# Block kernel on one core: an attention stage planned with other costs, banks and places for its side work

## The chip, the core and the metric

The kernel runs on one core of one Trainium2 chip, as one launch. The metric is the device time of that launch in microseconds (us). Three runs of the kernel before gave a median of 2030.43 us (2028.11 to 2034.91).

The core's engines run side by side, each through its own list of instructions in order: PE (matrix products; PEld is its loading of weights), DVE and ACT (elementwise work, both of which read the PSUM banks that PE writes), POOL (elementwise work on SBUF alone), and SP, which here issues the DMAs. An instruction that waits holds up everything behind it on its engine.

## The reference

All arithmetic is fp32. `xn` is the normalised input, and the result is `x + s * g`:

```python
x = A_x                                   # [1, 2048, 576]
xn = _layernorm(x, axis=-1)
# s: 32 heads of 18, a query sees itself and the 255 keys before it
q, k, v = heads(xn @ wqkv)
scores = einsum("bhqd,bhkd->bhqk", q, k) * (18 ** -0.5)
p = softmax(where((i - j >= 0) & (i - j < 256), scores, -1e9))
s = tokens(einsum("bhqk,bhkd->bhqd", p, v)) @ wo
# g: a gated MLP with a 2048 x 2048 mix over the tokens
z = gelu(xn @ w_in)                       # 4608 columns
z1, z2 = z[..., :2304], layernorm(z[..., 2304:])
g = silu((z1 * (w_sp @ z2 + b_sp)) @ w_out)
```

## The kernel before, in words

An fp32 factor is split into a high and a low part, and a product is three fast matmuls. ACT writes the high part and DVE or POOL the low part (`split` at line 108; `wq_high` and `wq_low` for the query/key weights; the jobs of `load_z1` for the z1 weights). The stages stand one after the other on PE, in microseconds of the profiled execution:

- 0 to 170: x is loaded in four chunks of four tiles, normalised (`stats_of` makes mean and variance, `scales_of` the factors, `norm_act` the normalised copy on ACT), turned by PE (`turn_group`), and multiplied by nine blocks of query/key weights. `fetch(j)` loads block j of these, three buffers deep. `keep_narrow` splits a product of 256 tokens and stores it with two DMAs.
- 170 to 464: the remaining query/key products, v, and z2. At the end of z2 the first row maxima of the attention are taken between z2's matmuls.
- 464 to 1044: the attention, with z1 as its filling. This is the stage that most of the change is about.
- 1044 to 1106: the product with `wo`. 1106 to 1794: the product of `w_sp` with z2. 1794 to 2028: the product with `w_out` and the result.

**The attention stage.** The work is cut into 16 units: 8 groups of four heads, by 2 halves of the queries. A unit first needs the row maxima. `max_item` (line 578) multiplies 128 queries with up to 384 keys into a bank of the pool `sps`, and DVE takes the masked maximum (line 582). After 32 of them `max_split` and `max_end` turn the maxima, and four small DMAs (line 608, `att<-mhl`) put them beside the queries as two further rows of the operand, so that the next product comes with its maximum already subtracted. Then `scores` (line 702) multiplies a block of keys with up to 384 queries into a bank of the pool `tps`, ACT takes the exponential (line 706), POOL cuts the corners of the mask (lines 714 and 717), and `pv` (line 730) multiplies by v. v holds a column of ones, so a row of each head's result is the denominator. `finish` brings the denominators to 128 partitions by DMA (`den`), DVE inverts them, a DMA writes them to `r_d`, another reads them back, spread over the partitions (`rp<-r_d`, line 774), DVE multiplies by them in two halves (line 781), and four DMAs store the unit (line 791).

Maxima, scores and z1 use half of PE's rows each. Heads 0 and 2 of a group lie in rows 0 to 63, heads 1 and 3 in rows 64 to 127, and two instructions on different halves run side by side. The products with v use all of PE. z1 is 18 blocks of weights (f) by 2 parts of the tokens by 27 matmuls on each half of the rows (`z1_rows`, line 649); a block's raw weights come by one DMA of 576 KB into a single buffer (line 618), and six jobs of ACT and POOL split them.

**What sets the order.** The order of all instructions is written when the program is built. For the attention stage a planner does so: a clock of its own advances by a cost for each instruction (`spend` for PE, `use` for ACT, DVE and POOL). At each step it takes, for the half of PE's rows that is free first, a score or a maximum if its operands and its bank should be there by that clock (`can_score`, `can_max`), and else a z1 matmul (`fill`). DMAs are registered with a due time (`after`) and issued when the clock has reached it (`tick`). `LOAD_NS` and `MAX_NS` are the times after which loaded queries and keys, and maxima, are taken to be there; `DIVIDE_AT` tells when a unit's divisions go in; `GUARD` is a margin of 150 ns. On the chip nothing follows that clock: the engines run their lists as fast as the waits let them.

The last unit's denominators are handled behind the loop, between the first products with `wo`.

## Time and profile before

| what | value |
|---|---|
| median of three runs | 2030.43 us |
| the profiled execution: its time, its span | 2029.56 us, 2027.8 us |
| PE busy, share of the span | 1925.4 us, 95% |
| mean granted clock of PE | 0.963 |
| DVE, ACT, POOL busy | 1061.5, 911.8, 354.8 us |
| attention, 464 to 1030 us: PE busy of 566 us, mean granted clock | 496.9 us, 0.91 |

The times are read from the span's start. A row of the waits names an engine and a line, what it waited for, the total in us, how often and the longest. In the table by stretches each engine has its busy time and in brackets the number of its instructions; PEclk is the mean share of PE's clock that was granted.

### The profile page before, as it was taken

To read this page: it belongs to the slowest core of one execution; us is meant where nothing else is said; L and a number is where in the kernel's file an instruction comes from. 1 tells how busy PE (TensorE), PEld (TensorE's weight loads), DVE (VectorE), ACT (ScalarE), POOL (GpSimd) and SP (SyncE) were. 2 spreads that over 40 slices of the span, in tenths; PEclk is the share of its full clock that TensorE was granted. 3 is DMA by queue.
4 is the path that set the end of the run, shared out by engine and by line. 5 is a ranking of instruction groups with operands and counts; after the bars stand their busy time and mean duration, and the time that the engine had idled before them with its cause. 6 is when DMAs were issued, how large, how long until landed. Compare 5 with 4: busy or idle time off the path is not lost.

```text
span 2027.8 us, 38429 instructions
## 1 busy us (share of the span) xinstructions
PE 1925.4 (95%) x14552; PEld 1654.0 (82%) x14552; DVE 1061.5 (52%) x2305; ACT 911.8 (45%) x1758; POOL 354.8 (17%) x424
## 2 busy tenths in 40 slices
PE   8799999999999878898899999999999999999999
PEld 7699999986676656566689888888888888899998
DVE  6420343556565445555322777756877576753322
ACT  4422322314554345455635856546556544442221
POOL 2222233433343224233410000000000000000000
PEclk8899999999998888989889999999999999999999
DMA  5686688886464644455356867766577655775451
GB/s 184 172 221 178 206 277 283 277 258 177 131 178 118 164 109 120 122 159 145 112 175 241 272 219 245 255 233 228 182 241 245 206 172 186 225 256 169 134 158 55
DMA packets 233353, 389.84 MB, mean 192 GB/s; under 512 B 51024, under 2 KB 144720, under 8 KB 233040
## 3 DMA queue, kind: packets, MB, share of 16 engines
q1 hardware_dynamic: 233168, 387.39, 61.9%
q8 instruction: 114, 1.87, 0.4%
q14 instruction: 71, 0.58, 0.1%
HBM read 274.74 MB, written 111.78 MB: 191 GB/s over the span
## 4 chain that ended last, share of the span: by engine, by line
PE 78%; DMA 9%; DVE 5%; ACT 3%; SPq 2%; issue 2%; POOL 0%; POOLq 0%; DVEq 0%; ACTq 0%
PE acc L1377 30%; PE po L1470 11%; PE mb L200 9%; PE ma L200 6%; PE ma L649 5%; PE mb L649 5%; PE ops L730 4%; PE wops L1137 3%; PE sp L578 2%; PE tps L702 2%; DMA z1raw<-in_w_z_dram 2%; DMA att<-st_d 2%; DVE junk L582 1%; DMA st_d<-qkhl 1%; SPq L346 1%
## 5 line engine op out<-in xcount | busy, mean ns | idle before, releaser
L582 DVE CUSTOM_DVE_ANT_0 junk<-sp,band 128x384 bf16<-128x384 f32 (+1 forms) x512 | 275.8, 539 | 232.5 <-PE sp L578 124.0
L1377 PE MATMUL acc<-spl,zh 128*128 128x512 f32 x1008 | 392.6, 389 | 1.2 <-DVE spl L110 1.0
L1377 PE MATMUL acc<-sph,zl 128*128 128x512 f32 x1008 | 392.2, 389 | 0.0
L1377 PE MATMUL acc<-sph,zh 128*128 128x512 f32 x1008 | 392.2, 389 | 0.0
L706 ACT ACTIVATE pt<-tps 128x384 f32<-128x384 f32 (+2 forms) x576 | 224.4, 443 | 165.4 <-PE tps L702 108.3
L649 PE MATMUL ma<-b,z1wh 64*128 64x512 f32 x648 | 238.4, 427 | 1.2 <-ACT z1o L654 0.7
L649 PE MATMUL mb<-b,z1wh 64*128 64x512 f32 x648 | 236.6, 422 | 1.8 <-ACT z1wh L664 1.8
L1377 PEld LDWEIGHTS acc<-spl,zh 128*128 128x128 f32 x1008 | 189.2, 188 | 42.0 <-DVE spl L110 2.9
L110 DVE TENSOR_TENSOR spl<-spr,sph 128x1024 fp32r<-128x1024 f32 x168 | 205.2, 1221 | 33.0 <-ACT sph L109 31.2
L1377 PEld LDWEIGHTS acc<-sph,zh 128*128 128x128 f32 x1008 | 189.3, 188 | 39.5
L1377 PEld LDWEIGHTS acc<-sph,zl 128*128 128x128 f32 x1008 | 189.3, 188 | 38.9
L702 PE MATMUL tps<-att 56*128 56x384 f32 (+1 forms) x576 | 178.4, 364 | 35.9 <-ACT pt L706 19.8
L578 PE MATMUL sp<-att 54*128 54x384 f32 (+1 forms) x512 | 184.4, 386 | 9.4 <-DMA att<-st_d 5.1
L109 ACT ACTIVATE zh<-b 128x384 fp32r<-128x384 f32 x168 | 87.4, 520 | 226.1 <-PE acc L1377 226.1
L109 ACT ACTIVATE sph<-spr 128x1024 fp32r<-128x1024 f32 x168 | 175.9, 1047 | 3.1 <-DMA spr<-sc_d 1.5
L110 DVE TENSOR_TENSOR zl<-b,zh 128x384 fp32r<-128x384 f32 x168 | 92.9, 553 | 146.8 <-ACT zh L109 146.8
L702 PEld LDWEIGHTS tps<-att 56*128 56x128 f32 x576 | 106.6, 205 | 60.1 <-issue 26.5
L1470 PE MATMUL po<-b,yh 128*128 128x288 f32 x840 | 147.1, 295 | 0.5 <-ACT gs L1457 0.5
L649 PE MATMUL mb<-b,z1wl 64*128 64x512 f32 x324 | 137.4, 424 | 2.5 <-POOL z1wl L645 2.5
L649 PE MATMUL ma<-b,z1wl 64*128 64x512 f32 x324 | 137.8, 425 | 0.0
L649 PEld LDWEIGHTS ma<-b,z1wh 64*128 64x128 f32 x648 | 127.6, 203 | 10.6 <-issue 3.9
L578 PEld LDWEIGHTS sp<-att 54*128 54x128 f32 x512 | 95.8, 196 | 48.7 <-DVE mx L582 23.6
(233 smaller groups left out, 4246.4 us busy)
## 6 DMA issues: line engine op xcount, KB each, us to landing
spr<-sc_d SPq DMA_DIRECT2D x96, 512.0 KB
spr<-in_w_sp_dram SPq DMA_DIRECT2D x72, 512.0 KB
zr<-z_d SPq DMA_DIRECT2D x144, 192.0 KB
z_d<-zt SPq DMA_DIRECT2D x48, 384.0 KB
z_d<-z1o SPq DMA_DIRECT2D x72, 256.0 KB
z1t<-z_d SPq DMA_DIRECT2D x72, 256.0 KB
y_d<-z1t SPq DMA_DIRECT2D x72, 256.0 KB
a<-in_w_sp_dram SPq DMA_DIRECT2D x64, 256.0 KB
```

The lines of the kernel that those rows point to most:

```text
L109: act.activation(hi, src, AF.Copy)
L110: dve.tensor_tensor(lo, src, f32(hi), ALU.subtract)
L200: pe.matmul(banks[h][:, :n], *both[h][i], start=i == 0, stop=i == STEPS - 1)
L578: pe.matmul(ps[:, :w], q_of(u, j)[0:54, i * P:(i + 1) * P], k_of(u, j)[0:54, k0:k0 + w], start=True, stop=True)
L582: dve.tensor_tensor_reduce(out=junk[:, :w], in0=ps[:, :w], in1=band[:, m0:m0 + w], scale=1.0, scalar=-3.0e38, op0=ALU.add, op1=ALU.max, ac ...
L649: pe.matmul(ps, w, x_, start=n == 0, stop=n == STEPS - 1)
L702: pe.matmul(ps[:, :m * P], k_of(u, j)[:, (kb - base) * P:(kb - base + 1) * P], q_of(u, j)[:, (a - lo) * P:(a - lo + m) * P], start=True, s ...
L706: act.activation(pt[:, j, d0:d0 + n * P], ps[:, (qa - a) * P:(qa - a + n) * P], AF.Exp, scale=scale)
L730: pe.matmul(o_ps[c][32 * j:32 * j + 32, (qa - 4 * c) * P:(hi - 4 * c + 1) * P], vgs[u][:, kb - k0, j * VW:j * VW + 32], pt[:, j, (qa - kb) ...
L1137: pe.matmul(po[:, i, :288], lt[:, cs], r[:, i * 288:(i + 1) * 288], start=n == 0, stop=n == len(pl) - 1)
L1377: pe.matmul(acc[j], z[:, ps], w[:, cs], start=s == i == 0 and n in OPENS, stop=s == 7 and i == 2, skip_group_check=True)
L1470: pe.matmul(po[i][:, a, :288], y if ahead else y[:, i * P:(i + 1) * P], w[a], start=f == 0 and m == 0, stop=f == NF - 1 and m == 2)
```

## The change

Seven things change:

- Banks: `sps` has three banks and `tps` two (before: two and three). The rules for taking a maximum or a score look back three and two results instead of two and three. The three banks also serve the maxima that are taken at the end of z2.
- Costs and due times of the planner: a maximum costs DVE 710 ns instead of 630, an exponential of 384 columns ACT 371 ns plus 125 ns until its result is there instead of 495, and so on; `LOAD_NS` and `MAX_NS` are 1500 ns longer.
- The divisions: on POOL, in four quarters, planned 18 to 22.5 us after the unit's end (DVE, two halves, 24 and 26 us). The reciprocal is planned at 7.5 us instead of 8, and the reading of `r_d` is four DMAs of 128 KB, each for 32 partitions, 400 ns apart, the first 3.5 us behind the store of the reciprocals, in place of one of 512 KB 4.8 us behind it. The last unit is divided on POOL in two halves.
- z1's raw weights of the next block are loaded at the first matmul of the block before, not at its ninth.
- Products with v are begun when seven (not four) blocks of 128 queries are ready.
- At the beginning, the statistics and factors of a chunk stand ahead of the splits of query/key products on DVE, and two of POOL's weight splits wait for the factors (`behind`). The loads of the weight blocks 5 to 8 and of the last chunk of x stand earlier.
- The factor `-mean * scale` is made with the scales instead of with the normalising.

```diff
-LOAD_NS = 4000
-MAX_NS = 3500
-DIVIDE_AT = (24000, 26000)
+LOAD_NS = 5500
+MAX_NS = 5000
+INVERT_AT = 7500
+FETCH_AT = 3500
+DIVIDE_AT = (18000, 19500, 21000, 22500, 23500, 24000, 24500, 25000)
+SPB = 3
...
             stats_of(1, range(4))
+            done = scales_of(1, range(4))
             fetch(4, w_qk[4])
...
             wq_high(3)
-            scales_of(1, range(4))
-            wq_low(3)
+            behind(wq_low(3), done)
...
             keep_narrow(2, 0, banks)
+            stats_of(2, range(4))
             wq_high(4)
             wq_low(4)
+            fetch(5, w_qk[5])
...
+            fetch(6, w_qk[6])
             keep_narrow(4, 0, banks)
             for j in range(5):
-                if j < 4:
-                    fetch(5 + j, w_qk[5 + j])
...
                 banks = narrow(j, 1)
+                if j < 2:
+                    fetch(7 + j, w_qk[7 + j])
...
-            sps = open_pool(ph, "sps", bufs=2, space=PSUM)
+            sps = open_pool(ph, "sps", bufs=SPB, space=PSUM)
...
-            def use(engine, ns):
+            def use(engine, ns, drain=0):
                 busy[engine] = max(busy[engine], clock + 200) + ns
-                return busy[engine]
+                return busy[engine] + drain
...
-                done_max.append(use("dve", 630 if w > 256 else 500))
+                done_max.append(use("dve", 710 if w > 256 else 580))
...
-                                bank_free[r] = use("act", 620) + 100
+                                bank_free[r] = use("act", 480, 120) + 100
...
-                                if b == 0 and n == 8 and f + 1 not in z1w:
+                                if b == 0 and n == 0 and f + 1 not in z1w:
                                     z1w[f + 1] = load_z1(f + 1)
...
-                done_exp.append(use("act", 180 + 105 * n))
+                done_exp.append(use("act", 53 + 106 * n, 125))
...
-                def get_inverse():
-                    sp.dma_start(rp, r_d[u].unsqueeze(1).to_broadcast([4, 32, HS]))
...
-                def divide_half(a):
-                    hs = slice(a * 512, a * 512 + 512)
-                    dve.tensor_tensor(ou[:, hs], ou[:, hs], rp[:, hs], ALU.mult)
-                    use("dve", 750)
...
+                    for i in range(4):
+                        after(t + FETCH_AT + 400 * i, partial(sums, i))
+
+                def sums(i):
+                    sp.dma_start(rp[32 * i:32 * i + 32, :], r_d[u][i:i + 1, :].to_broadcast([32, HS]))
+
+                def divide(a, n=4):
+                    hs = slice(a * HS // n, (a + 1) * HS // n)
+                    pool.tensor_tensor(ou[:, hs], ou[:, hs], rp[:, hs], ALU.mult)
+                    use("pool", 2400 / n)
...
-                tps = open_pool(heads, "tps", bufs=3, space=PSUM)
+                tps = open_pool(heads, "tps", bufs=5 - SPB, space=PSUM)
...
-                            and done_exp[-3] + GUARD <= clock)
+                            and done_exp[SPB - 5] + GUARD <= clock)
...
-                    return head_ready.get(2 * u + j // 2, 1e9) <= clock and done_max[-2] + GUARD <= clock
+                    return head_ready.get(2 * u + j // 2, 1e9) <= clock and done_max[-SPB] + GUARD <= clock
...
-                        return n if size >= 4 or len(pts) >= 4 or not score_queue[0] else 0
+                        return n if size >= 7 or len(pts) >= 4 or not score_queue[0] else 0
```

The change moves nearly every instruction of the attention stage. Three places are shown, each before and with the change. In the rows `att` is the operand buffer with queries, keys and maxima, `st_d` the stored queries and keys, `ou` a unit's result, `vg` a group's v, `z1o` a finished piece of z1, `ma` and `mb` z1's banks for the two halves of the rows. Line numbers of the changed kernel are some eleven higher.

SP's list around the load of the eleventh block of z1 weights (`z1raw`), before:

```order
L528 DMA att_2225<-st_d 36x1024
L528 DMA att_2225<-st_d 18x1280
L551 DMA z_d<-z1o 128x2x256
L528 DMA att_2225<-st_d 18x1024
L528 DMA att_2225<-st_d 36x1280
L618 DMA z1raw<-in_w_z_dram 128x1152
L791 DMA o_d<-ou 18x1024 x3
L803 DMA den<-ou 128x1x32
L791 DMA o_d<-ou 18x1024
L677 DMA vg<-v_d 128x10x89
L551 DMA z_d<-z1o 128x2x256 x2
L768 DMA r_d<-den 128x32
```

And with the change:

```order
L539 DMA att_2227<-st_d 36x1280
L792 DMA o_d<-ou 18x1024 x3
L629 DMA z1raw<-in_w_z_dram 128x1152
L562 DMA z_d<-z1o 128x2x256
L803 DMA den<-ou 128x1x32
L562 DMA z_d<-z1o 128x2x256
L688 DMA vg<-v_d 128x10x89
L562 DMA z_d<-z1o 128x2x256
L778 DMA r_d<-den 128x32
L619 DMA att_6846<-mhl 2x8x128 x2
L619 DMA att_6848<-mhl 2x8x128 x2
L783 DMA rp<-r_d 32x1024 x4
```

The load now stands ahead of the stores of the block before; a run of loads of queries and keys still stands ahead of it. `rp` is read by four DMAs.

PE's list at the end of the attention, before (33 more z1 matmuls on `ma` follow, then the first product with `wo`):

```order
L702 MATMUL tps<-att_2226 128x256
L649 MATMUL ma<-b_93,z1wh 128x512
L702 MATMUL tps<-att_2226 128x256
L730 MATMUL ops<-pt,vg 32x384 x4
L730 MATMUL ops<-pt,vg 32x256 x4
L730 MATMUL ops<-pt,vg 32x128 x4
L649 MATMUL ma<-b_96,z1wh 128x512
L649 MATMUL ma<-b_93,z1wl 128x512
L649 MATMUL ma<-b_94,z1wh 128x512
L649 MATMUL ma<-b_97,z1wh 128x512
L649 MATMUL ma<-b_94,z1wl 128x512
```

And with the change:

```order
L660 MATMUL ma<-b_97,z1wh 128x512
L660 MATMUL ma<-b_94,z1wl 128x512
L713 MATMUL tps<-att_2228 128x256
L741 MATMUL ops<-pt,vg 32x256 x4
L660 MATMUL ma<-b_94,z1wh 128x512
L660 MATMUL ma<-b_97,z1wh 128x512
L660 MATMUL ma<-b_94,z1wl 128x512
L741 MATMUL ops<-pt,vg 32x128 x4
L1137 MATMUL wops<-att_2229,ohl_14854 128x288 x2
```

Before, 38 z1 matmuls of one half of the rows stand behind the last product with v; now none does, and the product with `wo` follows it at once.

SP's list at the beginning, before (`qkhl` are split products, `wraw` raw weights, `xr` tiles of x):

```order
L258 DMA wraw<-in_w_qk_dram 128x1152 x3
L282 DMA xr<-in_x_dram 128x576 x4
L353 DMA st_d<-qkhl 64x2x512 x10
L258 DMA wraw<-in_w_qk_dram 128x1152
L282 DMA xr<-in_x_dram 128x576 x4
L353 DMA st_d<-qkhl 64x2x512 x2
L258 DMA wraw<-in_w_qk_dram 128x1152
```

And with the change:

```order
L261 DMA wraw<-in_w_qk_dram 128x1152 x3
L289 DMA xr<-in_x_dram 128x576 x4
L359 DMA st_d<-qkhl 64x2x512 x6
L261 DMA wraw<-in_w_qk_dram 128x1152
L359 DMA st_d<-qkhl 64x2x512 x2
L289 DMA xr<-in_x_dram 128x576 x4
L261 DMA wraw<-in_w_qk_dram 128x1152
```

The sixth block of weights is loaded behind six stores instead of ten, and the seventh behind eight instead of twelve.

## The prediction

> **What bounds the kernel now.** First the busy time of each engine by stage, in stretches cut at the stages' ends:

> ```profile
> 30.00:60.00 30.00, 23.34 (x348) 21.79 (x346) 14.81 (x44) 15.00 (x31) 7.47 (x3) 0.91 0.62 183
> 60.00:90.00 30.00, 23.09 (x255) 20.90 (x255) 15.61 (x37) 13.40 (x28) 8.71 (x4) 0.75 0.53 137
> 200.00:320.00 120.00, 120.00 (x1478) 120.00 (x1476) 40.88 (x67) 36.15 (x86) 42.37 (x42) 1.00 0.73 245
> 464.00:1030.00 566.00, 496.89 (x4348) 364.44 (x4348) 299.00 (x1054) 297.31 (x735) 200.94 (x291) 0.91 0.50 139
> 1030.00:1044.00 14.00, 13.31 (x38) 9.70 (x37) 3.65 (x5) 3.59 (x5) 0.00 (x0) 0.65 0.67 193
> 1044.00:1106.00 62.00, 62.00 (x451) 61.90 (x451) 12.88 (x16) 27.64 (x40) 0.00 (x0) 0.97 0.69 231
> 1106.00:1794.00 688.00, 686.76 (x3028) 567.59 (x3027) 481.95 (x680) 385.02 (x579) 0.00 (x0) 1.00 0.69 226
> 1794.00:2028.00 234.00, 229.20 (x1725) 228.73 (x1723) 79.94 (x140) 54.21 (x96) 0.00 (x0) 1.00 0.45 142
> ```

> After the stretch and its length come PE, PEld, DVE, ACT and POOL, then the granted clock, the DMAs' share and GB/s. The late stages and z2 keep PE busy at full clock, and the change leaves their work alone. PE has holes where the change works: 13.6 us between 30 and 90, and 566.0 - 496.9 = 69.1 us in the attention, where no other engine is over 53% busy. So waits bound that stage, not an engine. The clock goes with them: a mean of 0.91 from values of 1.0 and 0.5 is (1 - 0.91) / 0.5 = 18% of 566 us, 102 us at half rate.

> Then who waited in the attention:

> ```profile
> ACT z1wh L664 <- DMA z1raw<-in_w_z_dram: 52.9, 10, 13.7
> ...
> PE ops L730 <- ACT ou L745: 19.8, 13, 7.9
> PE tps L702 <- ACT pt L706: 19.8, 5, 7.3
> ...
> PEld sp L578 <- DVE mx L582: 19.2, 64, 0.6
> ...
> PE tps L702 <- DMA att<-mhl: 15.9, 9, 4.0
> ...
> DVE ou L781 <- DMA rp<-r_d: 7.6, 2, 7.0
> ...
> PE sp L578 <- DMA att<-st_d: 5.1, 3, 2.4
> ...
> PE mb L649 <- POOL z1wl L645: 2.5, 2, 1.5
> ...
> PE mb L649 <- ACT z1wh L664: 1.8, 1, 1.8
> ```

> The first row is the largest cause. ACT's list reaches the split of the next z1 block, its DMA has not landed, and the exponentials behind it stand still. PE then waits for an exponential or for the copy of a result. The chain of waits shows these loads, and three rows that are needed below (start, us, what):

> ```profile
> 533.78 4.72 DMA att<-st_d
> ...
> 681.23 7.63 DMA rp<-r_d
> ...
> 743.22 8.38 DMA z1raw<-in_w_z_dram
> ...
> 779.97 7.61 DMA z1raw<-in_w_z_dram
> ...
> 816.42 0.68 SPq L608
> ...
> 821.18 7.21 DMA z1raw<-in_w_z_dram
> ```

> PE's long holes stand there, and the clock falls with them:

> ```profile
> 740.00:760.00 20.00, 11.30 (x78) 9.80 (x78) 6.26 (x20) 7.27 (x20) 3.47 (x5) 0.66 0.56 143
> 780.00:796.00 16.00, 9.90 (x80) 7.59 (x71) 2.32 (x7) 5.84 (x16) 3.63 (x5) 0.68 0.77 193
> 820.00:834.00 14.00, 6.12 (x40) 4.47 (x37) 3.26 (x11) 4.62 (x14) 1.04 (x2) 0.76 0.62 169
> 898.00:904.00 6.00, 4.88 (x47) 3.57 (x43) 4.11 (x12) 4.25 (x14) 3.66 (x4) 1.00 0.80 194
> 904.00:908.00 4.00, 3.82 (x22) 3.71 (x24) 1.84 (x7) 1.58 (x4) 1.22 (x2) 0.58 0.77 222
> ```

> **The change, part by part.** *z1's weights sooner.* Of PE's holes I count to this cause the 19.8 us behind exponentials, the long ones behind `ou` (13 waits; if the others are about 0.8 us each, some 10 of the 19.8 us), and 2.5 + 1.8: together 34 us. The load now stands eight z1 steps earlier. A half of the rows makes 18 x 54 = 972 steps in the 580 us of the stage, 0.60 us each, so 21 steps between load and first use were 12.5 us; 29 steps at the quicker pace that I expect (0.54) are 15.7 us. 3.2 us more against a mean wait of 52.9 / 10 = 5.3 us takes some 56% away: -19 us. Bounds: 0, if the load is held up on SP by what it was held up by before, and -34.

> *Later due times.* PE waited 15.9 us in 9 times for the maxima's DMA and 5.1 in 3 for queries and keys. The planner now counts on both 1.5 us later and fills with z1 until then; there is z1 left to the last scores, as the end of PE's new list shows. 9 x 1.5 = 13.5 at most; I take -9 and -3. Bounds: 0 and -21.

> *Three banks for maxima, at their own pace.* Two maxima on DVE follow each other by 0.71 us:

> ```profile
> 690.72 0.56 DVE L582 CUSTOM_DVE_ANT_0 junk<-sp,band 128x384 bf16<-128x384 f32 x1 [1.13 <-PE sp L578]
> ...
> 691.43 0.56 DVE L582 CUSTOM_DVE_ANT_0 junk<-sp,band 128x384 bf16<-128x384 f32 x1
> ```

> The old plan wrote one every 0.63 us into two banks, hence 64 waits of the weight loads, 19.2 us. Each stops one half of PE's rows: worth up to 10 us, and I take -5 (bounds 0 and -10). What the third bank costs, the exponentials' third, is a rival below; with it their new rule waits for the result before last.

> *The clock.* Of the 102 us at half rate PE was busy for some 80% (56 to 96% in the stretches above), so 40 us are lost. Holes fall from 69 to 69 - 19 - 12 = 38 us, 45% less; the clock follows in proportion: -18. Bounds: 0 and -40. The row that decides: in 898 to 904 PE is idle for 1.1 us in all, and 904 to 908 has a clock of 0.58, so short holes cost clock too. [...]

> *The end of the stage.* After its last product with v PE had 38 z1 matmuls of one half alone, then `wo`:

> ```profile
> 1029.12 0.42 PE L730 MATMUL ops<-pt,vg 128*32 128x128 f32 x8 [0.46 <-POOL pt L714]
> ...
> 1036.71 1.27 ACT L1123 ACTIVATE ohl<-spare 128x1280 fp32r<-128x1280 f32 x1 [3.78 <-DMA o_d<-ou]
> ...
> 1038.01 1.23 DVE L1124 TENSOR_TENSOR ohl<-spare,ohl 128x1024 fp32r<-128x1024 f32 x1 [8.40 <-ACT ohl L1123]
> ...
> 1043.69 61.89 PE L1137 MATMUL wops<-att,ohl 128*128 128x288 f32 x448
> ```

> These 14 us (1029.5 to 1043.7, at a clock of 0.65) go. The 38 matmuls, 14 x 0.65 = 9 us at full clock, move into the stage, where both halves work: +4. Their cover goes with them: the first split for `wo` on ACT waits for the store of the unit before, so PE will stand still for that, 1.3 us of ACT and 1.7 of DVE: +6, estimated (bounds +2 and +10). Sum: -4.

> *Divisions on POOL.* The nearest rows (count | busy, mean ns | idle before):

> ```profile
> L664 POOL TENSOR_TENSOR z1wl<-z1raw,z1wh 128x384 fp32r<-128x384 f32 x26 | 25.8, 1011 | 14.1 <-ACT z1wh L664 14.1
> ...
> L781 DVE TENSOR_TENSOR ou<-ou,rp 128x512 f32<-128x512 f32 x30 | 21.7, 728 | 7.6 <-DMA rp<-r_d 7.6
> ```

> DVE loses 21.7 us of work that bounded nothing. POOL gains 60 quarters of 1011 x 256 / 384 = 674 ns, 40 us beside 201 in 566. Behind a quarter stand masks, and behind those the products with v; half a quarter of delay in each of 15 units is +5 (bounds 0 and 60 x 0.67 = 40). SP issues 45 DMAs more, at up to 0.68 us (the issue of `att<-mhl` in the chain): 2 us for each unit, mostly while SP waits anyway: +3 (bounds 0 and 31). The smaller number of products with v begun at once, the last unit's two halves on POOL (1.35 us each instead of 0.73, six products with `wo` ahead of their user) and the moved factor are taken as nothing: `wo`'s 62 us of busy PE cover them.

> *The beginning.* Between 30 and 90 PE lost 13.6 us in holes; at clocks of 0.91 and 0.75 it spent 20 us at half rate, with 77% busy another 8. ACT waited for weights, and a DVE instruction on four columns took 2.48 us while POOL's split ran:

> ```profile
> ACT wqh L262 <- DMA wraw<-in_w_qk_dram: 10.7, 3, 6.4
> ...
> 29.52 2.67 POOL L265 TENSOR_TENSOR wql<-wraw,wqh 128x1152 fp32r<-128x1152 f32 x1 [3.70 <-ACT wqh L262]
> ...
> 29.75 2.48 DVE L115 TENSOR_SCALAR st<-st 128x4 f32<-128x4 f32 x1
> ```

> Both causes are addressed: the loads pass four stores on SP, and the factors are made before POOL starts. POOL's split then waits for DVE, and other splits behind it; but the low weights are used in the last third of a product's matmuls, which covers a delay of 2 us. I take half of 21: -10 (bounds -2 and -18).

> **The sum**: -19 - 12 - 5 - 18 - 4 + 5 + 3 - 10 = -60 us. Against the profiled execution, span 2027.8 and time 2029.56 us, this gives 1969.6; the median of the runs lies 0.9 us above that execution, so **1970 us**, with 1945 to 1995 as this forecast's own range (each of the three largest terms a third off).

> **The rivals.**

> *The loads stay late* (0.2). SP's list is in order too. In the new list the z1 load still stands behind a run of loads of queries and keys, and what blocked SP there blocks it again. Against it: the load is now ahead of z1's stores, which wait for ACT. Then the first term is nothing and the clock's falls to 12 x 18 / 31 = 7: -60 + 19 + 11 = -30, 2000 us.

> *The holes collapse* (0.15). Every hole moves the engines away from the plan, so that later DMAs are late as well; with the first ones gone the others may not come. With the first two groups of waits at -50, the clock at -33, the rest as above (-11): -94, 1936 us.

> *POOL waits for the denominators* (0.06; the other side). The last of the four loads is planned 3.5 + 1.2 = 4.7 us behind the reciprocals' store, about 13 us after the unit's end, and the first quarter at 18: 5 us, where before 24 - 13.5 = 10.5 us were left, and DVE waited in 2 of 15 units all the same. If the load still takes 7.63 us, POOL stands 2.6 us in each unit, the masks and PE with it, 15 x 2.6 = 39 us, and with a stretch of 7 us at half rate behind each hole another 15 x 3.5 = 52: -60 + 91 = +31, 2061 us. It decides from a landing of about 6.5 us on. For a quick landing speaks the `att<-st_d` load, of similar size to a quarter of `rp`: 4.72 us. [...]

> *Two banks hold up the exponentials* (0.05). Each score waits for the exponential two before it. If the plan is off by 0.1 us in the 576 scores, half the rows stand for 58 us: +29, 1999 us. Against it: ACT is busy 297 of 566 us.

> *Nothing comes of it* (0.04). PE's time is then set by transfers that take what they take: 2029 us.

> **How the numbers follow.** The forecast has 0.5. A measurement of this kernel can tell some 0.3% (6 us) from no change. Faster by more than that are the forecast and the rivals at 2000, 1936 and 1999: 0.5 + 0.2 + 0.15 + 0.05 = 0.90. Within it 0.04, slower 0.06. The range reaches from 1930 to 2010: it leaves out the other side, no change, and the outer parts of the rivals at 1936 and 2000, together 0.2.

> **What would show it.** In the profile after: ACT's wait for `z1raw` at about 23 us instead of 52.9 (first term); PE's for `att<-mhl` below 8; the weight loads' for DVE near 0, and no new row of PEld waiting for `pt` of that size; a clock of 0.95 or more in the attention; `wo`'s first product about 6 us behind the last one with v; DVE's L115 row at 0.2 us in the first 100 us, and `wo` beginning some 60 us earlier. The prediction is wrong if POOL has a large wait for `rp`, if the `z1raw` row stands near 50, or if the attention's holes are as many under other names.

## The result, and the profile after

The changed kernel takes 1944.62 us (median of four runs, 1941.25 to 1949.88), the kernel before in the same series 2029.27 us. The ratio is 0.9585, with a 95% interval from 0.9549 to 0.962: 84.7 us faster, where 60 were predicted (1970 us, range 1930 to 2010). The profiled execution took 1941.25 us, with a span of 1939.5 us.

Three marks divide the spans of the two profiled executions. The first exponential begins at 458.6 us instead of 474.9 (16.3 us earlier). From there to the first product with `wo` it takes 494.7 us instead of 568.8 (74.1 us less). From there to the end it takes 986.2 instead of 984.1 us (2.1 us more). The gain lies in front of `wo`, most of it in the attention.

The busy time by stretches, as in the prediction (length, then PE, PEld, DVE, ACT, POOL, granted clock, the DMAs' share, GB/s), in the changed kernel:

```profile
30.00:60.00 30.00, 27.59 (x444) 26.66 (x442) 17.72 (x61) 18.76 (x39) 11.42 (x5) 0.89 0.85 242
60.00:90.00 30.00, 26.25 (x265) 23.73 (x263) 10.79 (x26) 15.15 (x32) 8.66 (x4) 0.94 0.66 153
...
449.00:943.00 494.00, 461.54 (x4344) 346.88 (x4342) 282.17 (x1017) 299.92 (x732) 236.90 (x348) 0.97 0.57 159
```

```profile
946.00:953.30 7.30, 0.00 (x0) 0.00 (x0) 0.01 (x1) 1.96 (x4) 0.00 (x0) 0.58 0.81 244
953.30:1017.00 63.70, 63.01 (x451) 61.95 (x452) 16.48 (x19) 28.20 (x40) 3.53 (x2) 0.97 0.71 226
```

In the attention PE is idle for 494 - 461.5 = 32.5 us instead of 69.1, and the clock is 0.97 instead of 0.91. That is (1 - 0.97) / 0.5 x 494 = 30 us at half rate instead of 102. A new hole of 7.3 us stands ahead of `wo`.

The waits in the stretch from 449 to 943 us of the changed kernel (total, times, longest):

```profile
PEld sp L589 <- DVE mx L593: 14.9, 30, 2.3
PE sp L589 <- DMA att<-st_d: 14.6, 8, 2.9
ACT z1wh L675 <- DMA z1raw<-in_w_z_dram: 12.7, 4, 5.8
...
PE tps L713 <- ACT pt L717: 7.7, 4, 4.1
...
POOL ou L787 <- DMA rp<-r_d: 3.7, 3, 1.7
...
PE tps L713 <- DMA att<-mhl: 2.6, 1, 2.6
...
PE ops L741 <- ACT ou L756: 1.3, 1, 1.3
```

ACT's wait for z1's weights has gone from 52.9 to 12.7 us, PE's for exponentials from 19.8 to 7.7, for copied results from 19.8 to 1.3 (the short ones among them too), for the maxima's DMA from 15.9 to 2.6. The wait for queries and keys, which the later due times were to take away, has grown from 5.1 to 14.6 us and is now PE's largest.

### The profile page after: what moved, and what is told of

Read it like the earlier page. It is cut to its first block, busy times and chain, and to the rows that moved or that the text cites. A ratio compares the mean times of both kernels' runs of the same rounds, so it can differ in the third digit from the quotient of the medians.

```text
span 1939.5 us, 38538 instructions
## 1 busy us (share of the span) xinstructions
PE 1876.8 (97%) x14552; PEld 1627.8 (84%) x14552; DVE 1038.2 (54%) x2275; ACT 914.3 (47%) x1758; POOL 397.6 (20%) x486
## 4 chain that ended last, share of the span: by engine, by line
PE 78%; DMA 9%; DVE 5%; SPq 3%; issue 2%; ACT 2%; POOL 1%; POOLq 0%; DVEq 0%; ACTq 0%
PE acc L1378 31%; PE po L1471 12%; PE mb L203 10%; PE ma L660 5%; PE ma L203 4%; PE mb L660 4%; PE ops L741 4%; DMA att<-st_d 3%; PE tps L713 2%; PE sp L589 2%; PE wops L1137 2%; DMA z1raw<-in_w_z_dram 1%; SPq L352 1%; DMA den<-ou 1%; DMA st_d<-qkhl 1%
## 5 line engine op out<-in xcount | busy, mean ns | idle before, releaser
L717 ACT ACTIVATE pt<-tps 128x384 f32<-128x384 f32 (+2 forms) x576 | 230.3, 439 | 151.3 <-PE tps L713 102.5
L660 PE MATMUL mb<-b,z1wh 64*128 64x512 f32 x648 | 228.2, 406 | 0.4 <-ACT z1o L665 0.3
L660 PE MATMUL ma<-b,z1wh 64*128 64x512 f32 x648 | 227.0, 406 | 0.5 <-ACT zt L935 0.4
L589 PE MATMUL sp<-att 54*128 54x384 f32 (+1 forms) x512 | 162.8, 359 | 19.5 <-DMA att<-st_d 14.6
L713 PEld LDWEIGHTS tps<-att 56*128 56x128 f32 x576 | 100.7, 189 | 41.9 <-ACT pt L717 16.6
L660 PE MATMUL ma<-b,z1wl 64*128 64x512 f32 x324 | 130.3, 402 | 0.0
L660 PE MATMUL mb<-b,z1wl 64*128 64x512 f32 x324 | 130.1, 402 | 0.0
L589 PEld LDWEIGHTS sp<-att 54*128 54x128 f32 x512 | 89.7, 189 | 45.1 <-issue 22.8
L660 PEld LDWEIGHTS ma<-b,z1wh 64*128 64x128 f32 x648 | 119.9, 190 | 6.6 <-issue 1.8
```

What stands on the lines that cost most here:

```text
L589: pe.matmul(ps[:, :w], q_of(u, j)[0:54, i * P:(i + 1) * P], k_of(u, j)[0:54, k0:k0 + w], start=True, stop=True)
L660: pe.matmul(ps, w, x_, start=n == 0, stop=n == STEPS - 1)
L713: pe.matmul(ps[:, :m * P], k_of(u, j)[:, (kb - base) * P:(kb - base + 1) * P], q_of(u, j)[:, (a - lo) * P:(a - lo + m) * P], start=True, s ...
L717: act.activation(pt[:, j, d0:d0 + n * P], ps[:, (qa - a) * P:(qa - a + n) * P], AF.Exp, scale=scale)
```

## The experiments

Every kernel was timed beside the kernel before, on the same chip. In the table the last three columns are from each kernel's profiled execution: when its first exponential begins, when its last product with v ends, and when its last z1 matmul ends. A difference between two of these kernels is the difference of their ratios times 2025 us; it carries both intervals, about 9 us where nothing else is said.

| kernel | median us | ratio, 95% interval | first exponential | last with v | last z1 |
|---|---|---|---|---|---|
| before | 2024 to 2029 | 1 | 474.9 | 1029.5 | 1043.8 |
| changed | 1944.62 | 0.9585 (0.9549 to 0.962) | 458.6 | 945.9 | 945.5 |
| 1: changed, z1's load late | 1945.84 | 0.9606 (0.9582 to 0.963) | 457.8 | 955.5 | 955.2 |
| 2: changed, old due times | 1941.96 | 0.9587 (0.9563 to 0.9612) | 458.9 | 944.6 | 964.3 |
| 3: changed, divisions on DVE | 1941.44 | 0.9585 (0.9561 to 0.9609) | 459.6 | 943.2 | 944.8 |
| 4: changed, old beginning | 1960.69 | 0.9667 (0.964 to 0.9695) | 470.4 | 966.6 | 966.3 |
| 5: changed, two banks for maxima | 1951.36 | 0.9637 (0.9618 to 0.9657) | 461.2 | 956.1 | 929.5 |
| 6: changed, old costs | 1968.07 | 0.9714 (0.9693 to 0.9736) | 458.5 | 971.7 | 949.9 |
| 7: before, z1's load early | 1994.81 | 0.9851 (0.9832 to 0.987) | 472.3 | 996.5 | 999.2 |
| 8: before, third bank and new costs | 1954.24 | 0.9653 (0.9637 to 0.9669) | 471.1 | 957.3 | 962.6 |
| 9: changed, four parts undone | 1948.2 | 0.9625 (0.9604 to 0.9646) | 458.0 | 946.4 | 947.3 |
| 10: changed, one load of `rp` | 1961.68 | 0.97 (0.9678 to 0.9723) | 461.8 | 961.4 | 961.1 |
| 11: before, exponentials' cost | 2009.4 | 0.9916 (0.989 to 0.9943) | 471.4 | 1009.0 | 1011.1 |
| 12: as 9, due times of 4.5 us | 1931.29 | 0.9536 (0.9514 to 0.9559) | 457.7 | 936.3 | 940.9 |

**1. z1's load back at the ninth matmul.**

```diff
-    if b == 0 and n == 0 and f + 1 not in z1w:
+    if b == 0 and n == 8 and f + 1 not in z1w:
```

> The changed kernel with z1's raw weights loaded at the ninth matmul of the block before again; only SP's list differs from the changed kernel. Theory A, the terms of the prediction add up: the z1 term (19 us) and its share of the clock term (18 x 19 / 31 = 11 us) come back, 1944.6 + 30 = about 1975 us; ACT's wait for z1raw near 50 us instead of 12.7. Theory B, the holes fed each other and the new costs of the plan already keep the loads in time: less than 8 us come back, about 1949 us, ACT's wait under 25 us.

1945.84 us. ACT's wait is doubled, from 12.7 to 24.4 us, and the time is 4 us longer (9 us uncertain), which can't be told from nothing:

```profile
ACT z1wh L675 <- DMA z1raw<-in_w_z_dram: 24.4, 4, 10.8
...
PE tps L713 <- ACT pt L717: 19.6, 4, 9.1
```

The profiled execution was the longest of five (1950.24 us), and in it PE does stand longer for exponentials: 19.6 us, 12 more than in the changed kernel. But ACT waits for z1's weights in 4 of 17 blocks here, where it did so ten times before. Theory B holds: with the rest of the change in place, the load is early enough at either place in most blocks.

**2. The old due times.**

```diff
-LOAD_NS = 5500
-MAX_NS = 5000
+LOAD_NS = 4000
+MAX_NS = 3500
```

> The changed kernel with the old due times (queries and keys 4.0 us, maxima 3.5 us). Theory A: the term of 12 us and its share of the clock term (18 x 12 / 31 = 7 us) come back, about 1963 us, with PE's waits for mhl near 12 us and for st_d near 20 us. Theory B: with fewer holes elsewhere these DMAs land in time anyway, or z1 that is used later covers as much: within 6 us of the changed kernel, 1939 to 1951 us.

1941.96 us, no difference. The waits are there, much as theory A had them:

```profile
PE sp L589 <- DMA att<-st_d: 25.3, 11, 3.5
PE tps L713 <- DMA att<-mhl: 7.0, 2, 5.2
```

They cost nothing on balance. The table shows what stands against them: z1 lasts until 964 us, beyond the last product with v, and fills most of the hole ahead of `wo` (whose first product comes 3.2 us behind the last with v instead of 7.4). What the later due times put between the scores, they take from the stage's end.

**3. The divisions on DVE,** in two halves at 24 and 26 us, with one load of `rp` at its old place and the reciprocal at 8 us (an extract).

```diff
-DIVIDE_AT = (18000, 19500, 21000, 22500, 23500, 24000, 24500, 25000)
+DIVIDE_AT = (24000, 26000)
...
-                    pool.tensor_tensor(ou[:, hs], ou[:, hs], rp[:, hs], ALU.mult)
-                    use("pool", 2400 / n)
+                    dve.tensor_tensor(ou[:, hs], ou[:, hs], rp[:, hs], ALU.mult)
+                    use("dve", 750)
```

> The changed kernel with the divisions on DVE in two halves at the old times, and one load of rp of 512 KB. Theory A: POOL's 5 us and SP's 3 us of the sum come off, about 1937 us. Rival: the quarters on POOL cost nothing and the quicker loads of rp gain, so that the old form is slower by up to 10 us, about 1950 us.

1941.44 us, the same ratio as the changed kernel. Neither the 8 us of cost nor a gain can be seen; the two expectations are not told apart, but the move itself is worth little.

**4. The old beginning.** The order of statistics, splits and loads of the first 170 us is as before; the rest is the changed kernel (an extract of the edit).

```diff
                 keep_narrow(2, 0, banks)
-                stats_of(2, range(4))
                 wq_high(4)
                 wq_low(4)
-                fetch(5, w_qk[5])
...
             for j in range(5):
+                if j < 4:
+                    fetch(5 + j, w_qk[5 + j])
```

> The changed kernel with the old beginning (order of statistics, splits and loads of the first 170 us). Theory A: the term of 10 us comes back, 1955 us. Rival: all 17 us by which the first load of z1 in the attention stood earlier come from the beginning, 1962 us; if part of them is due to the third bank for the maxima at the end of z2, it lies between the two and z2's end is unchanged.

1960.69 us, 16.6 us slower. The profile gives a part of it a place: PE's holes between 30 and 90 us are back,

```profile
30.00:60.00 30.00, 22.21 (x342) 20.37 (x342) 14.54 (x44) 14.54 (x30) 7.21 (x3) 0.96 0.63 181
60.00:90.00 30.00, 22.59 (x257) 20.99 (x255) 15.65 (x38) 14.03 (x28) 9.06 (x4) 0.76 0.54 138
```

and the first exponential comes 470.4 - 458.6 = 11.8 us later. Of the 16.3 us that this point moved, 11.8 belong to the beginning. The other 4 have no cause that is shown: the kernels of experiments 7 and 11 have the old beginning and two banks, as the kernel before has, and reach this point at 472.3 and 471.4 us, so most of the 4 may be a difference between executions. What the third bank gives the maxima at the end of z2 is about 1 us: from the first of them to the first exponential it takes 47.4 us in the changed kernel and 48.5 before. The remaining 5 us of the slowdown came in the attention, and the runs of this kernel scatter over 11 us, so that part is not explained.

**5 and 6. Two banks for maxima, or the old costs of the plan** (of the costs an extract).

```diff
-SPB = 3
+SPB = 2
```

```diff
-                done_max.append(use("dve", 710 if w > 256 else 580))
+                done_max.append(use("dve", 630 if w > 256 else 500))
...
-                done_exp.append(use("act", 53 + 106 * n, 125))
+                done_exp.append(use("act", 180 + 105 * n))
```

> The changed kernel with two banks for maxima and three for exponentials again, the new costs kept. Theory P, the new costs of the plan brought most of the gain in the attention: within 12 us of the changed kernel, up to 1957 us (the plan writes a maximum every 0.71 us, which DVE keeps up with in two banks). Theory K, the third bank brought it: 1985 us or more, with PEld's wait for DVE's maxima above 19 us.

> The changed kernel with the old costs of the plan (a maximum 630 ns, an exponential 495 ns, z1's copy 620 ns and so on), three banks and all else kept. Theory P: most of the attention's gain goes, 1985 us or more, with long waits of ACT for z1raw or of PE for mhl back. Theory K: within 12 us of the changed kernel.

1951.36 us, 10.5 us slower, and 1968.07 us, 26 us slower. The first agrees with theory P. The second fits neither theory: it loses a third of the attention's gain, and the long waits for z1's weights (11.8 us) and for the maxima (2.6 us) do not come back. What comes back is the half-array wait for maxima (22.5 us in 77 waits), and something that no table of waits names. The stretches at the stage's end show it, in the kernel with the old costs:

```profile
930.00:945.00 15.00, 15.00 (x149) 10.90 (x149) 0.28 (x1) 9.33 (x26) 7.12 (x11) 1.00 0.30 81
945.00:960.00 15.00, 12.60 (x83) 6.75 (x81) 3.77 (x5) 12.88 (x28) 6.33 (x11) 0.92 0.53 150
960.00:971.70 11.70, 10.29 (x67) 3.85 (x59) 0.92 (x1) 4.32 (x13) 5.74 (x9) 0.50 0.36 106
```

z1 is used up at 949.9 us, 22 us before the last product with v, and in the last 11.7 us the scores and products with v run without it at half clock: 67 matmuls, where 149 stand in the 15 us up to 945. So the filling should last at least as long as the scores. How much of the 26 us this is stays open: with two banks z1 ends even 26.6 us early, and only 10.5 us are lost. Before, z1 outlasted the last product with v by 14 us; in the changed kernel it ends 0.4 us ahead of it.

**7. Only z1's load moved, in the kernel before.** The edit is that of the change.

> The kernel before with z1's raw weights loaded at the first matmul of the block before, and nothing else. The prediction's terms: 19 us and 11 us of clock, 2025 - 30 = 1995 us, ACT's wait for z1raw near 23 us. If the loads only showed that the engines had drifted away from the plan: less than 10 us faster, the wait moving to other names.

1994.81 us against the 1995 forecast, and ACT's wait stands where the prediction had it:

```profile
ACT z1wh L664 <- DMA z1raw<-in_w_z_dram: 25.0, 8, 7.6
```

Alone, this part is worth its 19 us and their clock: 30.2 us by the ratio (26 to 34). On top of the rest it is worth 4 us, with 9 us of uncertainty (experiment 1).

**8. Only the third bank and the costs, in the kernel before.** The edits are those of the change to `SPB`, `use` and the numbers given to it.

> The kernel before with the three banks and the new costs, and nothing else (old due times, z1 at the ninth matmul, divisions on DVE, old beginning, four blocks for a run of products with v). The prediction's terms: 5 us and its part of the clock, some 8 us, and the end of the stage 4: about 2013 us. Theory of the drift (a plan that the engines can keep leaves the DMAs in time): the attention's gain nearly whole, about 1944 + 16 for the beginning = 1960 us, ACT's wait for z1raw under 25 us.

1954.24 us: 70 us faster, against the 13 or so that the prediction's terms give. The load of z1's weights stands at the ninth matmul here, as before, and yet

```profile
ACT z1wh L665 <- DMA z1raw<-in_w_z_dram: 2.0, 1, 2.0
```

52.9 us of waiting became 2.0 without the load being moved. So its place alone was not what made it late. PE's list tells what did, since it is in order: how far its two halves are with z1 at any place is the plan's doing. When the place of the load is reached, one half of the rows is ahead of the other by 11 to 42 z1 matmuls in the kernel before (median 30, over 16 blocks), here by 0 to 6. The load waits for the half that lags, but the first split goes in with the half that leads, from its 30th matmul on. With a lead of more than 20 matmuls it follows the load at the next place there is. On PE 1.9 us lie between the two places in the kernel before (median), and 11.8 us here. The low splits show the same. Before, 25 of 51 were made only when a half came to their block (line 645), and here all in advance (number; nanoseconds of one: least, median, most; first and last start):

```profile
L645 POOL TENSOR_TENSOR z1wl<-z1raw,z1wh x25: 993/1009/1497, 690.2 to 1000.4; 128x384 fp32r<-128x384 f32 x25
```

```profile
L665 POOL TENSOR_TENSOR z1wl<-z1raw,z1wh x51: 995/1013/1027, 466.3 to 933.9; 128x384 fp32r<-128x384 f32 x51
```

In experiment 7 the halves stay as far apart as before (median 31), and half of the wait stays too. In the other kernels the median lead is 10 or less: 10 with the old costs and three banks (experiment 6), 2.5 with the new costs and two banks (experiment 5). Over all 14 profiled executions ACT waited for z1's weights in 24 of the 38 blocks with less than 5 us between the two places, and in 5 of the 160 with 8 us or more.

The new order also ended most of the wait of the weight loads for maxima (19.2 us before, 2.1 here) and, to a lesser degree, that for the maxima's DMA (15.9 to 11.1), with the old due times.

**9. Four parts undone together:** experiments 1, 2 and 3 and products with v from four blocks on. The third bank, the costs and the beginning stay.

```diff
-                        return n if size >= 7 or len(pts) >= 4 or not score_queue[0] else 0
+                        return n if size >= 4 or len(pts) >= 4 or not score_queue[0] else 0
```

> The changed kernel with four of its seven parts undone together: z1's load at the ninth matmul, the old due times, the divisions on DVE with one load of rp, products with v from four blocks on. What stays are the third bank, the new costs and the new beginning. If these carry the whole gain: the ratio of the bank and costs alone (0.9653) less the beginning's 0.008, about 0.957 or 1939 us, no more than 6 us from the changed kernel. By the prediction's terms (19 and 12 us and their clock, 18 us, come back; 8 us of POOL and SP go): about 1985 us.

1948.2 us: 8 us slower by the ratios, just under what can be told, and far from 1985. Bank, costs and beginning carry 76 of the 84 us.

**10. `rp` by one load,** with the divisions on POOL at their new times.

```diff
-                    for i in range(4):
-                        after(t + FETCH_AT + 400 * i, partial(sums, i))
+                    after(t + FETCH_AT + 1200, partial(sums, 0))
...
-                    sp.dma_start(rp[32 * i:32 * i + 32, :], r_d[u][i:i + 1, :].to_broadcast([32, HS]))
+                    sp.dma_start(rp, r_d[u].unsqueeze(1).to_broadcast([4, 32, HS]))
```

> The changed kernel with rp read by one DMA of 512 KB at the place of the last of the four; the divisions stay on POOL at 18 us. The rival of the other side (POOL waits for the denominators), by the landing of about 8 us that the old form had: POOL stands some 2 to 3 us for rp in each unit, 30 to 45 us in all, and the kernel is slower by 15 us or more, 1960 us or above. Against it: the units' real times leave slack behind the plan, POOL's wait stays under 15 us and the time within 6 us of the changed kernel.

1961.68 us, 23 us slower than the changed kernel. Two of the five loads of `rp` in the chain of waits of this kernel, the slowest and the quickest (start, us, what), those in the chains of experiments 6, 4 and 2, which have the four loads, and POOL's wait here:

```profile
509.09 9.48 DMA rp<-r_d
...
885.88 3.48 DMA rp<-r_d
```

```profile
502.25 2.30 DMA rp<-r_d
```

```profile
574.61 2.56 DMA rp<-r_d
```

```profile
697.25 6.18 DMA rp<-r_d
```

```profile
POOL ou L786 <- DMA rp<-r_d: 29.9, 8, 5.7
```

One load of 512 KB takes 7.5 to 9.5 us in four of the five and 3.5 in one, a quarter of it 2.3 and 2.6 us in two rows and 6.2 in one. POOL stands 29.9 us instead of 3.7, and PE's waits for the masks of line 728 grow from 0.2 to 4.5 us. Of the 18 us between the two profiled executions 12.5 lie between the first exponential and the product with `wo`; 3.2 lie ahead of the first exponential, where the edit changes nothing. This is the rival of the other side: its wait is shown, its price is some 23 us (9 uncertain) and not the 91 that it had, and how POOL's wait becomes that time is not followed further. It takes the early divisions as well: with them on DVE at 24 us, one load costs nothing (experiment 3).

**11. Only the exponentials' cost, in the kernel before.**

```diff
-                done_exp.append(use("act", 180 + 105 * n))
+                done_exp.append(use("act", 53 + 106 * n) + 125)
```

> The kernel before with one number of the plan changed: an exponential costs ACT 106 ns a block and 53 ns, and 125 ns more until its result is there, instead of 180 + 105 ns of ACT's time; two banks for maxima and all else as before. If this cost alone set the pace of the plan: at least 30 us faster, 1995 us or less, with ACT's wait for z1raw halved. If the maxima's cost and their third bank are needed with it: less than 15 us faster, with PEld's wait for the maxima above 19 us and the long waits for z1raw still there.

2009.4 us: 17 us faster (5 us uncertain), between the two expectations. ACT's wait for z1raw fell to 19.0 us, but another took its place:

```profile
PE tps L702 <- DMA att<-mhl: 34.2, 12, 6.0
```

The two costs were wrong in opposite directions. On ACT three exponentials in a row take 1.25 us where one takes 0.49, one every 0.38 us, and the old plan counted 0.495:

```profile
596.03 1.25 ACT L706 ACTIVATE pt<-tps 128x384 f32<-128x384 f32 x3 [1.40 <-PE tps L702]
597.62 0.49 ACT L706 ACTIVATE pt<-tps 128x384 f32<-128x384 f32 x1 [0.33 <-PE tps L702]
```

On DVE a maximum comes every 0.71 us, and the plan counted 0.63. With the cost made right for ACT alone the maxima come later (34.2 us of waiting instead of 15.9). That the plan then runs further ahead of DVE would explain it, and is not shown.

**12. The parts that carry the gain, with due times between old and new.** As experiment 9, with

```diff
-LOAD_NS = 4000
-MAX_NS = 3500
+LOAD_NS = 4500
+MAX_NS = 4500
```

> As the kernel with four parts undone, but with due times between the old and the new (4.5 us for both): the list of PE then has some 5 us of z1 behind the last product with v, which cover part of the hole before the product with wo (7.4 us in the changed kernel), and PE's waits for mhl should lie between 2.6 and 11 us. Expected 3 to 8 us below the changed kernel, 1937 to 1942 us; if the due times don't matter, equal to the kernel with four parts undone.

1931.29 us, the fastest of all: 10 us below the changed kernel, with an uncertainty of 8.5, and 18 below experiment 9, with one of 6. From 449 to 936 us PE is idle for 28 us, against 34 there; the larger part is behind the last product with v:

```profile
936.00:941.00 5.00, 5.00 (x42) 3.67 (x35) 1.65 (x2) 1.88 (x2) 0.00 (x0) 1.00 0.74 209
```

```profile
PE sp L589 <- DMA att<-st_d: 12.0, 6, 5.1
PE tps L713 <- DMA att<-mhl: 11.2, 7, 3.2
```

z1 lasts until `wo` can begin, PE has no hole there, and the clock is 1.00. The changed kernel waits 7.4 us at this place and experiment 9 waits 8.7, each followed by slower products with `wo`: the first ten take 3.07 us there and the first 17 take 4.20 in experiment 9, where the 448 of the kernel before take 61.89 us, 0.14 each. The rest of both differences lies within their uncertainty or is not explained.

## Why the prediction was right or wrong

The range held, and what bounds the kernel was read rightly: waits in the attention, not an engine. The sum fell 25 us short: 1944.62 us lies at the lower edge of the forecast's own range (1945 to 1995), and inside the wider one, which reaches to 1930 for the sake of a rival. By its steps the account looks otherwise than it was written.

- **The three groups of waits (-19, -12, -5) were right as a sum, by luck, and wrong as parts.** PE's idle time in the attention fell by 36.6 us, where the terms give 36. But they were added up as though each wait had its own cause. The early load, for 19 us and its clock, is worth 30 us alone and 4 us beside the others; the later due times nothing beside the others (alone they were not tried, and experiment 12 gains 18 us on experiment 9 by due times in between); the third bank with the costs, for which 5 us stood, 70 us alone. What failed is the step from the first row of the waits: ACT's 52.9 us were put down to the place of the load, and experiment 8 took them away without moving it. The 21 steps and 12.5 us between load and first use hold only while the two halves of the rows are level; in the list before, 1.9 us (median) lie between them on PE. (3.2 us of 5.3 are also 60%, not 56; that moves the term by 1 to 2 us.)
- **The rival "the holes collapse" was nearer in its number (1936 us)** and had 0.15. It said that each hole moves the engines away from the plan, so that later DMAs are late. In experiments 7 and 8 two unlike edits each end much of the same waits, and the two gains (30 and 70 us) do not add up: with the 17 of the beginning they would make 117, and the whole change brings 84. That overlap is shown. For the largest wait the rival's mechanism is not what the traces show: in the kernel before, 16 loads of z1's weights were issued from 5.2 us ahead of PE's arrival at their place to 2.8 us behind it, and it was the plan itself that put the split close behind the load, by the lead of one half (experiment 8). For the waits for maxima a distance between plan and engines is argued, from the wrong costs on ACT and DVE and from experiment 11, and not measured. Why the old costs with two banks let one half run ahead, and which of the costs decides beside the exponentials', stays open.
- **The clock (-18) was the term most undersized.** At 40% lost of the time at half rate, as the prediction took it, 102 us make 40 and 30 make 12: -28. It was made proportional to the idle time, which fell by half; the time at half rate fell by 70%, and the holes that went were the long ones: those of 3 us and more went from 31.7 us in all to 4.1, the shorter ones from 37.4 to 28.3. Hole by hole the trace of the changed kernel shows no such proportion. Here is a hole of 1.94 us, ended at 491.9 us, that is followed by a stretch at half rate, and then one of 2.91 us, ended at 862.9 us, that is not:

```profile
489.71:493.13 3.42, 1.48 (x15) 1.28 (x14) 1.14 (x5) 1.31 (x3) 0.00 (x0) 1.00 0.70 174
493.13:496.54 3.41, 3.41 (x22) 3.33 (x21) 1.72 (x8) 1.57 (x4) 1.23 (x2) 0.50 0.85 214
858.35:861.77 3.42, 1.67 (x15) 1.23 (x11) 0.00 (x0) 1.96 (x5) 1.67 (x3) 1.00 0.67 184
861.77:865.18 3.41, 2.26 (x28) 1.66 (x30) 1.13 (x4) 1.02 (x3) 0.00 (x0) 1.00 0.75 160
865.18:868.59 3.41, 3.41 (x33) 2.80 (x34) 2.89 (x10) 3.03 (x7) 1.40 (x3) 1.00 0.95 200
```

- **The end of the stage (-4)** came out near the forecast: the 14 us of one half alone are gone, and a hole of 7.4 us stands in their place (6 were estimated). What the moved z1 matmuls cost inside the stage (4 were estimated) no run parts from the rest. The 14 us were the lead of one half again, this time at its end. The hole is the one that the prediction named:

```profile
945.46 0.43 PE L741 MATMUL ops<-pt,vg 128*32 128x128 f32 x8
953.31 3.07 PE L1137 MATMUL wops<-att,ohl 128*128 128x288 f32 x10 [7.43 <-ACT ohl L1123]
```

- **POOL's divisions and SP's issues (+5, +3)** cost nothing that experiment 3 can see. The rival behind them was real, and decided by the loads: with one load POOL waits 29.9 us (experiment 10), with four 3.7 us in all. Two of the three quarters shown under experiment 10 land far sooner (2.30 and 2.56 us against 7.5 to 9.5 in four of the five whole loads), the third does not (6.18 us). What makes them quicker the rows don't show: the shape of a load changed together with its size, 512 to 128 KB.
- **The beginning (-10)** measures 11.8 us to the first exponential, by experiment 4. Its mechanism is seen in the factors, made ahead of POOL's split. Two such instructions took 2.48 and 2.40 us before, 2.47 and 2.40 us with the old beginning in experiment 8 (2.40 and 2.33 in the chain of waits of experiment 4), and none of their kind takes over 0.3 us in the changed kernel. The row of 2.48 us (line 115, now 118) has become

```profile
27.31 0.14 DVE L118 TENSOR_SCALAR st<-st 128x4 f32<-128x4 f32 x1
```

- **Left out of the sum:** the third bank for the maxima at z2's end, about 1 us, and what the stage needs to end well, that z1 lasts as long as the scores. The prediction saw the tail only as an item of 14 us; experiment 6 shows a stretch at half clock where z1 has run out early, and experiment 12 that the same balance is worth the hole ahead of `wo`.
- **Of the signs that were named,** the wait for z1raw (about 23 forecast, 12.7 found), that for mhl (below 8: 2.6) and the clock (0.95: 0.97) came out better. The weight loads' wait for DVE (near 0 forecast) is 14.9 us in 30 waits; their wait for exponentials, which gave up a bank, is not larger than before (16.6 us in 29 waits, 23.0 in 8 before). `wo` begins 90 us earlier, not 60.

The profiled executions add up so: 16 us up to the first exponential (11.8 of them the beginning's), 37 of holes and 28 of clock in the attention, 3 at its end, less 2 from `wo` on: 82 of their 88 us. Of the rest up to 4 us may lie in the rounding of the two clocks, where 0.005 is 5 us at half rate and 2 us lost.

## What to carry to other kernels

Where in-order lists follow a plan, compare the plan's cost of each operation with the spacing of such operations in the trace before shortening any wait. Look in the lists, too, for how much work really lies between a load and its first use: a wait for a DMA may only say that the plan put them side by side. And two cures of one wait are not worth their sum. Filling work must last as long as the work it fills and then cover what the next stage waits for; both too much and too little of it showed here as a low clock at the stage's end, 0.65 in the kernel before and 0.50 in experiment 6. With one broadcast load in place of four of the same bytes in all this kernel was 23 us slower (9 us uncertain), and POOL, which has other work behind it, waited 29.9 us for the landing instead of 3.7.

## What the runs showed of the hardware

In the profiled executions of the kernel before and of the changed kernel the stretches at half clock were 3.41, 6.83, 10.24 or 13.65 us long (but for the last one of each, which the end of the execution cuts off): 3.41 us from 493.13 in the rows above, and 10.2 us behind the hole ahead of `wo`, beginning 1.2 us into the hole and lasting 4 us beyond its end:

```profile
941.00:947.10 6.10, 4.88 (x45) 2.07 (x42) 0.00 (x0) 2.61 (x8) 3.59 (x6) 1.00 0.55 156
947.10:957.30 10.20, 3.99 (x15) 3.71 (x16) 3.50 (x5) 2.43 (x2) 0.00 (x0) 0.50 0.67 205
957.30:960.70 3.40, 3.40 (x28) 3.40 (x27) 0.00 (x0) 1.25 (x2) 0.00 (x0) 0.99 0.89 289
```
